# Fixed pieces of one tile and four double PSUM banks in place of tile pools, in a kernel with two spectral and two state-space layers

## The chip, the cores and the metric

The kernel runs on one core of one Trainium2 chip. The metric is the device time of one execution in microseconds (us), lower is better, as the median of several executions.

## The reference

An activation x of 2048 rows and 512 columns goes through four layers, each with a layer norm and a residual:

```
x = x + A(layernorm(x))
x = x + B(layernorm(x))
x = x + A(layernorm(x))
x = x + B(layernorm(x))

A(x):  irfft2(rfft2(x) * (w_r + 1j*w_i))                     # filter over both axes
B(u):  K[d,l] = Re sum_n C[d,n] * exp(dt*A[d,n]*l) * dt*B[d,n]
       irfft(rfft(pad(u)) * rfft(pad(K)))[:2048] + u*Dskip   # long convolution along the rows
```

All is float32. Both layers B use the same kernel K, so its spectrum is computed once.

## The kernel before

All Fourier transforms are matmuls with tables of cosines and sines, in two steps each, with the twiddle factors in the second step's table. A first part builds the spectrum of K (`setup_k`, 32 times `unit_k` on `exp_k`'s result, then `store_k`, `turn_k`, `spectra_k`); it needs x nowhere and runs beside the first layer A (index r = 0). Then follow layer B (r = 0), layer A (r = 1) and layer B (r = 1).

Layer A is `forward_a` (16 blocks of 128 rows), `first_a` or `group_a` (16 groups of frequencies) and `inv_a` (16 blocks). In `inv_a` four matmuls (L732) go to PSUM, ScalarE copies them out (L735), one matmul (L740) follows, ScalarE copies again (L743), and GpSimd and VectorE add the block to x.

Layer B is done in two column halves, e = 0 and e = 1.
- `forward_b`, 8 blocks b for each half: VectorE normalises two row blocks into a tile (L511), TensorE transforms them by eight matmuls (L781), four to each of two PSUM banks; ScalarE copies each bank out (L783), and the block is stored to DRAM in a new layout (L799, from SP's queue for even b, from ScalarE's for odd b). Matmuls of fp32 are in the trace with two records each, so a block of eight shows as x16. For r = 0 and e = 0 the two banks are one tile of 1024 elements, `pa`; else they are two tiles `px`.
- `group_b`, 16 groups q for each half: four matmuls to `px` (L811 and L812, with the tables `gi` and the rows of x's transform), two VectorE products with the spectrum `kh` (L873), two GpSimd sums (L879), four matmuls (L886) to the two banks `ph` and `pt`, and two ScalarE copies back (L892). For r = 0 and e = 1 the spectrum is computed in the same place from loads `yk` and `gk` (L853, L854) by matmuls on the same lines L811 and L812 and a copy (L860); else it is loaded (L864).
- `inv_b`, 8 blocks for each half: a load from DRAM (L901), eight matmuls to `ph` and `pt` (L908), and two VectorE adds to x (L914).
- `tables(r)` loads the 16 tables `gi` (L838), 256 KB each.

Nothing is written in a fixed order. Each of these functions is a generator whose pieces a list scheduler, the class `Clock`, takes one after the other: it keeps modelled times for each engine and takes the ready piece of the lowest rank. A piece yields what it needs before the next step: an engine, slots by name (`"PE p:h p:t"` is PE and a PSUM slot of the kinds h and t), and events. `Clock.tile` hands out the slot that the model takes to come free first; the order in which the pieces are taken is the order of the program on each engine's queue.

Memory is of two sorts. Some names are rings: fixed slices of tiles that stand for the whole program, with a table of sizes and counts for each (`RING`, `RINGA`, ...). The others (`a`, `iy`, `kh`, `yk`, `gk`, `KT`, `yh`, ...) and all of PSUM are allocated from tile pools, one new tile object for each use, with so many buffers for each tag. There are two such scopes one after the other, `w1` for the first 16 `forward_a` up to `forward_b` e = 0, and `w2` for all that follows. In PSUM `w1` has three double banks `a` and two single banks `s`; `w2` has four single banks `x`, two `t` and two `h`.

The waits on semaphores come from the framework: it compares the regions that each instruction reads and writes, and at the end of a pool's scope whatever takes its memory waits for all that used the pool.

Of the kernel before, what the change touches and what calls it, by code (L numbers as in the profile page):

```python
# [6 lines left out]
F32 = mybir.dt.float32  # L7
F32R = mybir.dt.float32r
BF = mybir.dt.bfloat16
# [1 line left out]
AF = mybir.ActivationFunctionType  # L11
OP = mybir.AluOpType

BUFS1 = {'yh': 3, 'KT': 3, 'st': 2, 'gb': 2}

RINGW = {"y": (514, 2), "b": (256, 2), "d": (256, 2), "c": (256, 2), "a": (512, 2)}
BUFS2 = {'a': 3, 'iy': 4, 'kh': 5, 'yk': 4, 'gk': 4}
BANKS1 = {'s': 2, 'a': 3}

SAME1, TWO = {'t': 's', 'h': 's', 'l': 's', 'x': 's', 'k': 'a'}, ('a',)  # L20
BANKS2 = {'t': 2, 'x': 4, 'h': 2}

RING = {"M": (3072, 3), "E": (3072, 2), "sq": (512, 2)}
RING0 = {"an": (3072, 1), "F": (2048, 1), "W": (1024, 2), "U": (1024, 2), "k": (512, 3), "hi": (1024, 2), "hj": (256, 2), "th": (512, 1), "ld": (4, 1),
         "dt": (4, 1)}
RINGX = {"G": (1284, 5), "t1a": (514, 1), "t2a": (514, 1), "Za": (520, 1)}

RINGG = {"G": (1798, 4), "tp": (128, 3)}
RINGA = {"G5": (1798, 1), "AB": (516, 3), "V": (516, 2), "t1a": (516, 2), "t2a": (516, 2), "Za": (516, 2)}
RINGB = {"gi": (512, 16)}  # L30

RINGC = {"b": (256, 3), "c": (256, 3), "d": (256, 3), "y": (512, 2), "yh": (512, 2)}
RINGD = {"t1": (512, 3), "t2": (512, 3), "Z": (512, 3)}
# [8 lines left out]
RANK = -4, 0.3, 6, 1.2, 25, 0.5, 24, 0.5  # L42

NEAR = 0.1


PSUM = bass.MemoryType.PSUM
# [4 lines left out]
MAGIC = 1.5 * 2.0 ** 23  # L52
# [130 lines left out]
class Clock:  # L183
# [4 lines left out]
    def __init__(self, net, last=None):  # L188
        self.net, self.n = net, len(net.nc.cur_bb.bb.instructions)
        self.free, self.seen, self.events, self.marks, self.drops = {}, {}, {}, [], []  # L190
        self.held, self.slots, self.land, self.piece, self.table, self.form = {}, {}, 0.0, None, "", None
        if last:
            self.free, self.seen, self.events, self.land, self.table = last.free, last.seen, last.events, last.land, last.table

            self.held = {k: h for k, h in last.held.items() if h[0] == "gi"}
            self.slots["gi"] = last.slots["gi"]

    def tile(self, name, make, count):

        slots = self.slots.setdefault(name, [(0.0, i) for i in range(count)])  # L200
        assert slots, name
        slots.sort()
        t, i = slots.pop(0)
        tile = make(i)
        self.held[self.key(tile)] = name, i, self.piece, tile
        if name not in self.net.ring:
            self.seen[tile.tensor.name] = [(self.boxes(tile), t, True)]
        return tile

    @staticmethod  # L210
    def key(tile):
        return tile.tensor.name, tile.offset * mybir.dt.size(tile.dtype)

    def drop(self, tile):
        self.drops.append(self.key(tile))
# [139 lines left out]
    def run(self, plan):  # L355

        pieces = [[rank, i, 0.0, (), piece] for i, (rank, piece) in enumerate(plan)]
        while pieces:
            ready = [(t, p) for p in pieces if (t := self.time(p[2], p[3])) is not None]
            assert ready, [p[4].__name__ for p in pieces]  # L360
            now = min(t for t, _ in ready) + NEAR
            t, p = min((e for e in ready if e[0] <= now), key=lambda e: e[1][:2])
# [13 lines left out]
class Net:  # L376
    def __init__(self, tc, io, ctx):
        self.tc, self.nc, self.io, self.ctx = tc, tc.nc, io, ctx
        self.const = self.pool("const", 1)
        self.big = self.pool("big", 1)  # L380
        self.ps = None
        nc = self.nc
        self.x = self.big.tile([128, 16, 512], F32, name="x")
        self.Ya = self.big.tile([128, 8192], F32, name="Ya")
        self.Y = self.big.tile([128, 16384], F32, name="Y")

        self.Yf = self.Ya, self.Y[:, :8192]

        self.place = [a.rearrange("p (g m) -> p g m", g=16) for a in (self.Y[:, 8192:], self.Ya)]
        self.eps = self.const.tile([128, 1], F32, name="eps")  # L390
        nc.vector.memset(self.eps, 1e-5)
        self.sm = self.pool("sm", 4)
        self.wk = None

    def pool(self, name, bufs, space=None):
        kw = {"space": space} if space is not None else {}
# [7 lines left out]
    def psum(self, kind):  # L404
        kind = self.same.get(kind, kind)

        def make(_):
            return self.ps.tile([128, 1024 if kind in TWO else 512], F32, name="p" + kind, tag="p" + kind, bufs=self.banks[kind])
        return self.timer.tile("p:" + kind, make, self.banks[kind])

    def drop(self, *tiles):

# [10 lines left out]
    def emitted(self, key, n=1):  # L423
        return self.timer.emitted(key, n)

    def work(self, name, bufs, **banks):

        net = self

        class Scope:  # L430
            def __enter__(scope):
                scope.cm = net.tc.tile_pool(name=name, bufs=1)
                net.wk = scope.cm.__enter__()
                scope.pm = net.tc.tile_pool(name=name + "p", bufs=1, space=PSUM)
                net.ps = scope.pm.__enter__()
                net.banks, net.bufs = banks, bufs

            def __exit__(scope, *a):
                net.wk = net.ps = None
                scope.pm.__exit__(*a)  # L440
                return scope.cm.__exit__(*a)
        return Scope()

    def w(self, name, shape, dt=F32):
        if name in self.ring:
            t = self.ring[name]
            t = self.timer.tile(name, t.__getitem__, len(t))
            t = t[:shape[0], :int(np.prod(shape[1:]))]
            if len(shape) > 2:
                names = "abcdef"[:len(shape) - 1]  # L450
                t = t.rearrange(f"p ({' '.join(names)}) -> p {' '.join(names)}", **dict(zip(names, shape[1:])))
            return t
        bufs = self.bufs.get(name, 1)

        def make(_):
            return self.wk.tile(list(shape), dt, name=name, tag=name, bufs=bufs)
        return self.timer.tile(name, make, bufs)


    def loads(self):  # L460
# [370 lines left out]

    def tables(self, r):

        for q in range(16):
            yield "SP gi", self.emitted(("inverse", 1), 16) if r else self.after("product", 32)
            self.gi[r, q] = self.w("gi", [128, 4, 128])
            self.timer.keep(self.gi[r, q])
            self.nc.sync.dma_start(self.gi[r, q], self.io["cGb"][q])  # L838
            self.mark("gi", r, q)
# [97 lines left out]
        self.nc.sync.dma_start(self.an[:, 2:6], self.io["kN"][:, 2:6])  # L937

    def load_h(self):
        cs = self.wk.tile([128, 5120], F32, name="cs")  # L940
        self.ring["yd"] = [cs[:, 1024 * i:1024 * i + 1024] for i in range(5)]
        self.ring["co"], self.ring["si"] = self.ring["yd"][:3], self.ring["yd"][3:]
        self.oh = self.wk.tile([128, 2560], BF, name="oh")[:96]
        self.nc.sync.dma_start(self.oh, self.io["cH"])

    def turns_of(self, out, t, n, k):
# [225 lines left out]
    def run(self):  # L1172
        self.khat = self.pool("khat", 1, DRAM).tile([128, 16, 2, 512], F32, name="khat")
        self.spe = self.pool("spe", 1, DRAM).tile([3, 2, 128, 1024], BF, name="spe")
        self.spt = self.pool("spt", 1, DRAM).tile([3, 128, 512], BF, name="spt")
        self.sq, self.st, self.gi = {}, {}, {}
        self.kd = self.pool("kd", 1, DRAM).tile([4, 4, 2048, 32], F32, name="kd")
        self.yk = self.pool("yk", 1, DRAM).tile([2, 16, 8, 4, 4, 2, 256], F32, name="yk")
        self.ring = {}
        self.same = SAME1  # L1180
        with self.work("w1", BUFS1, **BANKS1):
            wa = self.wk.tile([128, 3588], F32, name="wa")

            self.nc.vector.memset(wa[:, 64:64 + 514 + 1:514], 0.0)
            self.rings((RINGB, self.Y), (RING, self.Y), (RING0, self.Y), (RINGX, self.x.rearrange("p s d -> p (s d)")), (RINGW, wa))
            for name, value in (("magic", MAGIC), ("quarter", np.pi / 2)):
                t = self.const.tile([128, 1], F32, name=name)
                self.nc.vector.memset(t, value)
                setattr(self, name, t)
            sb = {}  # L1190
            self.timer = Clock(self)
            self.timer.run([(0, self.loads()), *self.plan_k(), *self.plan_a(sb)])
        self.same = {}
        with self.work("w2", BUFS2, **BANKS2):
            wb = self.wk.tile([128, 4608], F32, name="wb")
            self.ring = {"gi": self.ring["gi"]}
            self.rings((RINGG, self.Y[:, 8192:]), (RINGA, self.Ya), (RINGC, wb), (RINGD, wb))
            self.ring["G"] += self.ring.pop("G5")
            self.timer = Clock(self, self.timer)
            self.timer.run(self.plan_rest(sb))  # L1200

    def rings(self, *tables):

# [128 lines left out]
```

## Time and profile before

| | |
|---|---|
| median of 3 executions | 912.03 us (908.24 to 914.18) |
| profiled execution | 911.37 us |
| span of its trace | 909.6 us |
| mean granted TensorE clock | 0.941 |
| TensorE matmul busy | 711.0 us (78%) |
| TensorE weight loads | 501.4 us (55%, beside the matmuls) |
| VectorE busy | 562.9 us (62%) |
| ScalarE busy | 443.2 us (49%) |
| GpSimd busy | 374.2 us (41%) |
| DMA engines, queues of SP and ScalarE | 40.4% and 11.3% |

The span is shorter than the time by 1.8 us, which lie around it. Rows of the trace name a line (L886), an engine, the operation, and the tiles written and read with the shapes; "[9.35 <-X]" is the idle time of the engine ahead of the row, and what ended it.

### The profile page before, as it was taken

Reading aid. Unit: us, or ns where it says so; the run is one execution under the profiler, and the core shown is the slowest. Engines: PE = TensorE matmul, PEld = TensorE weight load, DVE = VectorE, ACT = ScalarE, POOL = GpSimd, SP = SyncE. Lnnn points to the kernel's source line nnn. Section 1 sums busy time; section 2 is a strip of 40 time slices with the busy share of each in tenths; the row PEclk is TensorE's granted clock in tenths of the full one; section 3 lists DMA queues with packets and bytes.
Section 4 is the critical chain, followed back from the end, with each engine's and each line's share of the span. In section 5 each row is a group of like instructions: output and inputs, shape, how many; then the busy total and the mean of one; then the engine's idle time right before and its main releaser. Section 6 shows DMA issues by size and latency. Waiting matters only on the chain.

```text
span 909.6 us, 17039 instructions
## 1 busy us (share of the span) xinstructions
PE 711.0 (78%) x6434; PEld 501.4 (55%) x6434; DVE 562.9 (62%) x1094; ACT 443.2 (49%) x817; POOL 374.2 (41%) x420
## 2 busy tenths in 40 slices
PE   0058888678878988973899978897887978599977
PEld 0046665355555645641656745696676645366646
DVE  6986887477475758761344534695884857566432
ACT  2458878776757667641344213286442444322210
POOL 0046665274353546631134215273443633166330
PEclk9999999999989889996899999899998989999998
DMA  9042025413413854557978994802540144767938
GB/s 327 32 148 75 13 78 185 122 61 123 155 53 128 267 135 132 175 163 173 272 190 235 260 347 140 216 3 78 207 163 1 47 93 127 181 200 197 268 85 228
DMA packets 91856, 138.39 MB, mean 152 GB/s; under 512 B 6812, under 2 KB 61344, under 8 KB 91136
## 3 DMA queue, kind: packets, MB, share of 16 engines
q1 hardware_dynamic: 59520, 107.95, 40.4%
q10 hardware_dynamic: 32256, 29.37, 11.3%
q8 instruction: 51, 0.84, 0.4%
q14 instruction: 29, 0.24, 0.1%
HBM read 76.60 MB, written 27.13 MB: 114 GB/s over the span
## 4 chain that ended last, share of the span: by engine, by line
PE 29%; DMA 9%; DVE 5%; ACT 3%; POOL 2%; issue 2%; SPq 1%; ACTq 0%; DVEq 0%; POOLq 0%
PE ph L886 6%; PE px L811 4%; PE px L781 3%; PE ph L908 3%; PE pt L732 3%; DMA iy<-Y 3%; PE px L812 3%; DMA Y<-iy 3%; DMA iy<-Ya 2%; DMA gk<-in_cGk_dram 2%; POOL Ya L622 1%; PE ph L740 1%; PE ph L631 1%; DVE Ya L617 1%; DVE Ya L618 1%
## 5 line engine op out<-in xcount | busy, mean ns | idle before, releaser
L879 POOL TENSOR_TENSOR wb<-wb 128x256 f32<-128x256 f32 x128 | 89.7, 729 | 159.2 <-DVE wb L873 119.7
L873 DVE TENSOR_TENSOR wb<-px,kh 128x512 f32<-128x512 f32 x128 | 80.9, 685 | 83.8 <-PE px L812 32.4
L1084 POOL TENSOR_TENSOR Y<-cs,Y 128x1024 f32<-128x1024 f32 x32 | 76.7, 2397 | 62.2 <-issue 29.6
L908 PE MATMUL ph<-iy,cRbT 64*128 64x256 f32 x256 | 67.2, 411 | 15.9 <-DMA iy<-Ya 13.3
L886 PE MATMUL ph<-wb,Y 64*128 64x256 f32 x256 | 70.9, 400 | 1.7 <-POOL wb L879 1.6
L886 PE MATMUL pt<-wb,Y 64*128 64x256 f32 x256 | 71.5, 401 | 0.0
L908 PE MATMUL pt<-iy,cRbT 64*128 64x256 f32 x256 | 66.5, 410 | 0.9 <-DVE x L914 0.9
L908 PEld LDWEIGHTS ph<-iy,cRbT 64*128 64x128 f32 x256 | 49.6, 202 | 25.2 <-issue 14.4
L781 PE MATMUL px<-a,cRb 128*64 128x256 f32 x384 | 50.8, 406 | 14.5 <-DMA Y<-in_cGb_dram 9.4
L886 PEld LDWEIGHTS ph<-wb,Y 64*128 64x128 f32 x256 | 42.7, 186 | 27.8 <-POOL wb L879 17.0
L1037 PE MATMUL pa<-oh,Y 96*128 96x512 bf16 x128 | 39.9, 389 | 22.9 <-DVE Y L1081 9.3
L1069 DVE SCALAR_TENSOR_TENSOR cs<-cs,pa 128x1024 f32<-128x1024 f32 x32 | 38.9, 1215 | 30.3 <-ACT cs L1067 30.1
L550 PE MATMUL ps<-cRa,wa 128*128 128x128 f32 x64 | 13.5, 294 | 55.9 <-POOL wa L535 55.2
L783 ACT COPY iy<-px 128x512 f32<-128x512 f32 x48 | 28.1, 586 | 56.8 <-PE px L781 56.7
L1080 DVE TENSOR_TENSOR Y<-pa,Y 128x1024 f32<-128x1024 f32 x32 | 39.0, 1219 | 21.9 <-ACT pa L1073 21.8
L908 PEld LDWEIGHTS pt<-iy,cRbT 64*128 64x128 f32 x256 | 49.9, 202 | 4.5 <-DVE x L914 3.1
L781 PEld LDWEIGHTS px<-a,cRb 128*64 128x64 f32 x384 | 32.9, 145 | 32.4 <-issue 16.5
L1072 ACT ACTIVATE cs<-cs,quarter 128x1024 f32<-128x1024 f32 x32 | 36.7, 1148 | 24.4 <-DVE cs L1070 22.6
L1053 ACT ACTIVATE Y<-pa 128x1024 f32<-128x1024 f32 x48 | 47.1, 1044 | 1.8 <-PE pa L1037 1.2
L914 DVE TENSOR_TENSOR x<-x,ph 128x256 f32<-128x256 f32 x32 | 13.4, 420 | 53.5 <-PE pt L908 43.0
L1097 PEld LDWEIGHTS ps<-Y 128*32 128x32 f32 x2048 | 33.8, 119 | 18.1 <-POOL Y L1085 8.5
L886 PEld LDWEIGHTS pt<-wb,Y 64*128 64x128 f32 x256 | 42.7, 186 | 0.2
(233 smaller groups left out, 1981.2 us busy)
## 6 DMA issues: line engine op xcount, KB each, us to landing
kh<-khat SPq DMA_DIRECT2D x48, 256.0 KB
Y<-in_cGb_dram SPq DMA_DIRECT2D x32, 256.0 KB
iy<-Y SPq DMA_DIRECT2D x16, 512.0 KB
iy<-Ya SPq DMA_DIRECT2D x16, 512.0 KB
Y<-in_W_dram SPq DMA_DIRECT2D x13, 515.0 KB
x<-in_cPa_dram SPq DMA_DIRECT2D x16, 384.0 KB
yk<-yh ACTq DMA_DIRECT2D x24, 256.0 KB
Y<-in_cGa_dram SPq DMA_DIRECT2D x13, 384.0 KB
```

The costliest lines, as they stand in the source:

```text
L781: self.nc.tensor.matmul(p[64 * s:64 * s + 64, 256 * h:256 * h + 256], self.Rb[:, 2 * h + j, :], xn[s], start=True, stop=True)
L811: self.nc.tensor.matmul(Xr[o], gb[:, j, 0:64], y[:, j, :], start=True, stop=True)
L873: nc.vector.tensor_tensor(t[c], X[:, c, None, :].to_broadcast([128, 2, 256]), k, op=OP.mult)
L879: nc.gpsimd.tensor_tensor(Z[:, c], t[0][:, c], t[1][:, c], op=op)
L886: nc.tensor.matmul(v[j], gi[o, 2 + c, :], Z[o, c, :], start=c == 0, stop=c == 1)
L908: nc.tensor.matmul(q[s], self.RbT[o, i, :], y[o, i, :], start=i == 0, stop=i == 3)
L1037: self.nc.tensor.matmul(p, f[:, c:c + 128], self.oh[:k, o:o + 512], start=True, stop=True)
L1053: nc.scalar.activation(m[:, :, 1024:] if i == 2 else m[:, i, :1024], p.rearrange("p (i m) -> p i m", i=2) if i == 2 else p, AF.Exp)
L1069: nc.vector.scalar_tensor_tensor(s, c, MAGIC, p, op0=OP.subtract, op1=OP.subtract)
L1072: nc.scalar.activation(c, c, AF.Sin, scale=-TURN, bias=self.quarter)
L1080: nc.vector.tensor_tensor(E[:, 1, :1024], p, m[:, :1024], op=OP.mult)
L1084: nc.gpsimd.tensor_tensor(E[:, 0, :1024], c, m[:, :1024], op=OP.mult)
```

## The change

The pools of the two scopes go. One tile `wk` of 128 x 17152 floats and four PSUM tiles `ps` of 128 x 1024 floats (two banks each) are allocated once. All names become rings on `wk`: RING1 behind RINGW for the first stage, RINGC, RINGD (one over the other) and RING2 for the second. Three counts grow: `gb` from 2 to 3 slots, `yk` and `gk` from 4 to 5. A single PSUM bank is now the left or the right half of a double tile: `s` the halves of the tile 3; `x` the four halves of the tiles 0 and 1, `t` those of the tile 2, `h` those of the tile 3. With one tile for both stages there is no end of a pool between them; an instruction of the second stage waits for those of the first whose regions it overlaps. In `tables` the condition is asked once, ahead of the loop, and the "+" in the yield lets each load follow the last without waiting for the modelled landing of the one before.

```diff
-BUFS1 = {'yh': 3, 'KT': 3, 'st': 2, 'gb': 2}
+RING1 = {"yd": (1024, 5), "oh": (1280, 1), "KS": (2048, 1), "KT": (512, 3), "yh": (512, 3), "gb": (256, 3), "st": (256, 2), "sk": (128, 1)}
...
-BUFS2 = {'a': 3, 'iy': 4, 'kh': 5, 'yk': 4, 'gk': 4}
-BANKS1 = {'s': 2, 'a': 3}
-
-SAME1, TWO = {'t': 's', 'h': 's', 'l': 's', 'x': 's', 'k': 'a'}, ('a',)
-BANKS2 = {'t': 2, 'x': 4, 'h': 2}
+RING2 = {"a": (512, 3), "iy": (1024, 4), "kh": (512, 5), "yk": (512, 5), "gk": (256, 5), "sk": (128, 1)}
+
+BANKS1, SAME1 = {'a': (0, 2, 4), 's': (6, 7)}, {'t': 's', 'h': 's', 'l': 's', 'x': 's', 'k': 'a'}
+BANKS2 = {'x': (0, 1, 2, 3), 't': (4, 5), 'h': (6, 7)}
...
         self.held[self.key(tile)] = name, i, self.piece, tile
-        if name not in self.net.ring:
-            self.seen[tile.tensor.name] = [(self.boxes(tile), t, True)]
         return tile
...
-        self.ps = None
+        self.ps = [self.pool("ps", 1, PSUM).tile([128, 1024], F32, name="ps%d" % i) for i in range(4)]
+        self.wk = self.big.tile([128, WORK], F32, name="wk")
...
     def psum(self, kind):
         kind = self.same.get(kind, kind)
 
-        def make(_):
-            return self.ps.tile([128, 1024 if kind in TWO else 512], F32, name="p" + kind, tag="p" + kind, bufs=self.banks[kind])
-        return self.timer.tile("p:" + kind, make, self.banks[kind])
+        banks = self.banks[kind]
+
+        def make(i):
+            p = self.ps[banks[i] // 2]
+            return p if kind == "a" else p[:, 512 * (banks[i] % 2):512 * (banks[i] % 2) + 512]
+        return self.timer.tile("p:" + kind, make, len(banks))
...
+        yield self.emitted(("inverse", 1), 16) if r else self.after("product", 32)
         for q in range(16):
-            yield "SP gi", self.emitted(("inverse", 1), 16) if r else self.after("product", 32)
+            yield "+SP gi"
             self.gi[r, q] = self.w("gi", [128, 4, 128])
```

The instructions are the same but for one table load on ScalarE. Their order differs between about 170 and 560 us of the trace; behind that, in layer A (r = 1) and layer B (r = 1), each of the four computing engines has the same order as before, and only the slots and the waits differ.

On SP's queue at the end of the first stage (line numbers of the changed kernel are lower by 21 to 24: L838 is L817, L799 is L777, L864 is L843, L1115 is L1091, L1126 is L1102) there stood

```order
L838 DMA Y<-in_cGb_dram 128x512 x2
L1115 DMA kd<-KS 128x2048
L838 DMA Y<-in_cGb_dram 128x512 x3
L799 DMA Y<-cs 16x8x1024
L838 DMA Y<-in_cGb_dram 128x512
...
L838 DMA Y<-in_cGb_dram 128x512 x8
L1126 DMA yk<-kd 128x4x128
L864 DMA kh<-khat 128x2x256 x3
```

(where the line of dots stands, the pair of one L799 and one L838 comes twice more, and then a fourth L799), and now

```order
L817 DMA Y<-in_cGb_dram 128x512 x16
L1091 DMA kd<-wk 128x2048
L777 DMA Y<-wk 16x8x1024 x4
L1102 DMA wk<-kd 128x4x128
L843 DMA wk<-khat 128x2x256 x3
```

All 16 tables now stand ahead of the four stores of `forward_b` blocks; before, eight of them stood behind the last.

On TensorE the last two blocks of `forward_b`, r = 1, with the tiles' numbers and the semaphores that each row waits for, stood before as

```order
L781 MATMUL px_6361<-a_6354,cRb_158 64x256 [waits DVE_49,Activation_49]
L781 MATMUL px_6361<-a_6354,cRb_158 64x256 [waits DVE_49]
L781 MATMUL px_6361<-a_6354,cRb_158 64x256 x2
L781 MATMUL px_6362<-a_6354,cRb_158 64x256 [waits Activation_49]
L781 MATMUL px_6362<-a_6354,cRb_158 64x256 x3
```

and now as

```order
L759 MATMUL ps0_66<-wk_79,cRb_166 64x256 [waits DVE_49] x2
L759 MATMUL ps0_66<-wk_79,cRb_166 64x256 x2
L759 MATMUL ps0_66<-wk_79,cRb_166 64x256 [waits Activation_49]
L759 MATMUL ps0_66<-wk_79,cRb_166 64x256 x3
```

The matmuls are the same and in the same order. Before, the second four write a tile of their own, and their wait on ScalarE is for the copy that emptied that bank an earlier time; now both fours write halves of the one tile ps0, and by its value the second four's wait on ScalarE is for the copy of the first four's result in the other half (the copy that the block's first four release).

More of the change, by code (lines that the diff above doesn't have):

```diff
@@ L44 @@
 NEAR = 0.1
+WORK = 17152
 PSUM = bass.MemoryType.PSUM
@@ L392, in __init__ @@
         self.sm = self.pool("sm", 4)
-        self.wk = None
     def pool(self, name, bufs, space=None):
@@ L424, in emitted @@
         return self.timer.emitted(key, n)
[L426 to L442, printed above, removed]
-    def w(self, name, shape, dt=F32):
[L445 to L457, printed above, removed]
+    def w(self, name, shape, dt=F32):
+        t = self.ring[name]
+        t = self.timer.tile(name, t.__getitem__, len(t))
+        t = (t if dt is F32 else t.bitcast(dt))[:shape[0], :int(np.prod(shape[1:]))]
+        if len(shape) > 2:
+            names = "abcdef"[:len(shape) - 1]
+            t = t.rearrange(f"p ({' '.join(names)}) -> p {' '.join(names)}", **dict(zip(names, shape[1:])))
+        return t
     def loads(self):
@@ L939, in load_h @@
     def load_h(self):
[L940 to L943, printed above, removed]
+        self.oh = self.ring["oh"][0].bitcast(BF)[:96]
         self.nc.sync.dma_start(self.oh, self.io["cH"])
@@ L1179, in run @@
         self.ring = {}
[L1180 to L1200, printed above, removed]
+        self.banks, self.same = BANKS1, SAME1
+        n = sum(n * k for n, k in RINGW.values())
+        self.nc.vector.memset(self.wk[:, 64:64 + 514 + 1:514], 0.0)
+        self.rings((RINGB, self.Y), (RING, self.Y), (RING0, self.Y), (RINGX, self.x.rearrange("p s d -> p (s d)")), (RINGW, self.wk),
+                   (RING1, self.wk[:, n:]))
+        self.ring["co"], self.ring["si"] = self.ring["yd"][:3], self.ring["yd"][3:]
+        for name, value in (("magic", MAGIC), ("quarter", np.pi / 2)):
+            t = self.const.tile([128, 1], F32, name=name)
+            self.nc.vector.memset(t, value)
+            setattr(self, name, t)
+        sb = {}
+        self.timer = Clock(self)
+        self.timer.run([(0, self.loads()), *self.plan_k(), *self.plan_a(sb)])
+        self.banks, self.same = BANKS2, {}
+        self.ring = {"gi": self.ring["gi"]}
+        n = sum(n * k for n, k in RINGD.values())
+        self.rings((RINGG, self.Y[:, 8192:]), (RINGA, self.Ya), (RINGC, self.wk), (RINGD, self.wk), (RING2, self.wk[:, n:]))
+        self.ring["G"] += self.ring.pop("G5")
+        self.timer = Clock(self, self.timer)
+        self.timer.run(self.plan_rest(sb))
     def rings(self, *tables):
```

## The prediction

> **What bounds the kernel now.** I first read the windows, the busy time of each engine by 40 us (start and end; PE, PEld, DVE, ACT, POOL with instruction counts; granted TensorE clock; DMA share; GB/s), because the change lies in several stages with different limits.
>
> ```profile
> 400.00:440.00 40.00, 20.10 (x127) 12.01 (x125) 9.01 (x26) 9.78 (x18) 2.28 (x3) 0.71 0.81 202
> 440.00:480.00 40.00, 38.60 (x268) 23.17 (x266) 17.46 (x31) 16.42 (x38) 14.17 (x21) 0.99 0.87 219
> 480.00:520.00 40.00, 39.51 (x329) 28.46 (x327) 19.30 (x37) 12.94 (x32) 15.22 (x22) 1.00 0.93 257
> 800.00:840.00 40.00, 39.85 (x320) 25.52 (x319) 25.33 (x41) 11.64 (x36) 28.63 (x41) 1.00 0.75 216
> 880.00:910.00 30.00, 17.82 (x132) 15.09 (x128) 6.02 (x16) 0.65 (x2) 0.00 (x0) 0.86 0.83 210
> ```
>
> Both layers B (440 to 560 and 796 to 866 us) are bound by TensorE: it is busy for 38.6 to 39.9 of 40 us, so whatever makes it wait there is added to the end nearly in full. Between them lies the boundary of the two stages, 400 to 440, the worst stretch: TensorE is busy for half of it. The tail from 880 is set by loads (DMA share 0.83) and has slack on TensorE.
>
> The timeline there, by engine (start, duration, engine, line, tiles, count, idle time ahead and its end):
>
> ```profile
> 423.34 0.54 SPq L799 DMA_DIRECT2D Y<-cs  x1
> 423.93 10.54 SPq L838 DMA_DIRECT2D Y<-in_cGb_dram  x8
> 434.61 2.03 DVE L511 TENSOR_SCALAR a<-x,mv,rs 128x256 f32<-128x256 f32 x6 [15.95 <-DMA Y<-in_cGb_dram]
> 435.12 9.92 PE L781 MATMUL px<-a,cRb 128*64 128x256 f32 x64 [9.35 <-DMA Y<-in_cGb_dram]
> 444.72 0.75 PE L811 MATMUL px<-Y 128*64 128x256 f32 x4
> ```
>
> The first instruction of the second stage, L511 into `a`, waits 15.95 us, TensorE then 9.35. The last even store leaves at 423.34, eight table loads behind it. The program of before makes L511 wait for all that used the first stage's pool, the last stores among them.
>
> **The boundary: a gain.** In the changed program L511 waits only for the stores whose regions it overlaps, of which that of 423.34 is the last, and the 16 tables have gone ahead of it. How long a store of this size takes without those loads is in the chain of waits (start, us, what), at the end of layer A (r = 1), which I need again below:
>
> ```profile
> 716.00 1.90 PE px L781 x16
> 725.07 3.63 PE px L781 x32
> 728.73 0.59 ACT iy L783
> 734.55 4.32 DMA Y<-iy
> ...
> 786.37 3.91 PE px L781 x31
> ...
> 790.31 5.25 DMA Y<-iy
> ...
> 795.69 1.13 PE px L811 x4
> ```
>
> So the store lands at about 423.34 + 4.32 = 427.7, and L511 starts 434.61 - 427.7 = 6.9 us earlier. Before, four `forward_b` blocks (x64) then stand ahead of the first L811; in the new order only two, each 9.92 / 4 = 2.48 us here, so L811 comes 6.9 + 5.0 = 11.9 us earlier. The two others are paid later, at 1.9 us each (the row x16 at 716.00): 11.9 - 3.8 = **8 us gained**. Bounds: 2 us, if the spectra `kh`, which are loaded behind the same stores, come late; 12, if the two blocks fall into holes. At the second boundary the store of 790.31 took 5.25 us beside three table loads that now stand ahead of it; at 4.32 it gives **1 us**. Together -9.
>
> [...]
>
> **PSUM halves: a loss.** Each single bank is now half of a tile, and the program's waits go by tile: an instruction that touches one half waits for another engine's last access to the other half too. By resolving the semaphore values of both built programs I count 585 waits whose instruction named touches only the other part of a PSUM tile, against 139 before. The trace of before already shows what one costs, since `pa`, the double tile of `forward_b` (r = 0, e = 0), has it and `px` does not. The groups (busy us, mean ns, idle us ahead and what ended it), the waits (us, times, longest) and a piece of the timeline:
>
> ```profile
> L781 PE MATMUL px<-a,cRb 128*64 128x256 f32 x384 | 50.8, 406 | 14.5 <-DMA Y<-in_cGb_dram 9.4 <-DVE a L511 5.2
> L781 PE MATMUL pa<-wa,cRb 128*64 128x256 f32 x128 | 19.6, 429 | 12.2 <-DVE wa L511 6.7 <-ACT cs L783 5.5
> PEld pa L781 <- ACT cs L783: 9.5, 8, 1.5
> 402.32 1.95 PE L781 MATMUL pa<-wa,cRb 128*64 128x256 f32 x16 [0.69 <-ACT cs L783]
> ```
>
> With `pa`, 8 blocks lose 5.5 us of matmul time to the copy of their own first half, 0.69 each; with `px`, 24 blocks lose none to it. [...]
>
> Now by line, with the copies' and adds' groups:
>
> ```profile
> L892 ACT COPY Y<-ph 128x256 f32<-128x256 f32 x32 | 11.9, 373 | 49.1 <-PE pt L886 47.7 <-ACT iy L1146 1.2 <-PE ph L886 0.2
> L914 DVE TENSOR_TENSOR x<-x,ph 128x256 f32<-128x256 f32 x32 | 13.4, 420 | 53.5 <-PE pt L908 43.0 <-PE ph L908 10.4
> L557 ACT COPY Ya<-ps 128x512 f32<-128x512 f32 x16 | 16.7, 1051 | 5.1 <-PE ps L553 5.0
> ```
>
> `forward_b`: the 24 `px` blocks now behave as `pa`. Eight (r = 0, e = 1) lie in the stretch where TensorE is the bound: 8 x 0.69 = 5.5. Of the 16 of r = 1, 12 are in the chain of waits (10 pieces, the first and the last of them at 716.00 and 786.37): 12 x 0.69 = 8.3. **+14**; bounds 5.5 (the first eight alone) and 24 x 0.69 = 16.6.
>
> `group_b`: here the timeline decides, at 816 us, where two groups follow each other and then a product:
>
> ```profile
> 816.06 0.48 PE L886 MATMUL ph<-wb,Y 64*128 64x256 f32 x1
> 817.03 0.38 PE L886 MATMUL ph<-wb,Y 64*128 64x256 f32 x1
> 817.22 0.37 ACT L892 COPY Y<-ph 128x256 f32<-128x256 f32 x1 [1.44 <-PE pt L886]
> 817.68 0.38 PE L886 MATMUL pt<-wb,Y 64*128 64x256 f32 x1
> 818.36 0.38 ACT L892 COPY Y<-pt 128x256 f32<-128x256 f32 x1
> 819.01 0.48 PE L886 MATMUL ph<-wb,Y 64*128 64x256 f32 x1
> 829.30 1.29 DVE L873 TENSOR_TENSOR wb<-px,kh 128x512 f32<-128x512 f32 x2 [1.66 <-POOL wb L879]
> 830.18 0.66 PE L811 MATMUL px<-Ya,Y 128*64 128x256 f32 x4
> ```
>
> The copies of the first group, begun at 817.22, now wait for the second group's matmuls in the other half, till 817.68 + 0.38 = 818.06, and the last of the four copies ends some 0.6 us later than at 818.74; the next group's start at 819.01 moves by about 0.3. Where a product stands between groups, as usual, nothing is lost. The other new wait is L811 for L873's reads of the other half: 829.30 + 1.29 = 830.59 against 830.18, 0.4 us. Over 812 to 832 us I find three such delays of TensorE, 0.4 to 0.7, in 9 groups: 1.7 / 9 = 0.2 each. For all 64 groups **+13**. Bounds: 0, and both copies in full ahead of every group, 64 x 2 x 0.375 = 48; I stay near the stretch counted.
>
> `inv_b`: 24 of 32 blocks now wait for the adds of the block before in the other half, at most 0.42 + 0.40 us. Half of them lie in the tail, which the loads set. **+4**; bounds 0 and 24 x 0.82 = 20.
>
> The first stage and layer A (r = 1): `s` is two halves of one tile, so `forward_a`, `first_a`, `inv_a` and the units lose some of their double buffering (L550 waits for L557's copy of the other half, 1.05 us, in 14 places, the copy for L553 in 15). But TensorE is less full there,
>
> ```profile
> 240.00:280.00 40.00, 31.19 (x414) 21.67 (x414) 25.32 (x38) 26.15 (x34) 18.30 (x12) 0.91 0.16 46
> 640.00:680.00 40.00, 33.70 (x286) 28.09 (x282) 33.82 (x92) 17.70 (x67) 18.26 (x27) 0.96 0.57 197
> ```
>
> 31 and 34 of 40 us, so that part falls into idle time, and the order up to 440 is another, which may help or hurt. **+5**; bounds -5, and 29 x 1.05 = 30.
>
> More slots for `yk` and `gk`: the chain holds one wait on a load,
>
> ```profile
> 530.07 9.86 DMA gk<-in_cGk_dram
> 540.06 1.13 PE px L811 x4
> ```
> ```profile
> L811 PE MATMUL px<-yk,gk 128*64 128x256 f32 x64 | 10.9, 408 | 5.5 <-DMA gk<-in_cGk_dram 5.5
> ```
>
> for which TensorE idles 5.5 us (the group's row). The load's place on SP is the same, behind the layer A loads; I take 0, bounds -5.5 and 0. `gb` lies in the first stage's terms. What the scheduler no longer notes for fresh tiles changes only the order.
>
> **Sum:** -9 + 14 + 13 + 4 + 5 = +27 us on the profiled execution's 911.4, 938; the median of the runs is 912.0, 0.6 above, so **939**.
>
> **Rivals.** *The waits are hidden.* The copies are short beside ScalarE's idle time (L892's group: 49 us idle), and TensorE, ordered as before, may find them done. For it speaks that most groups have a product between them; against it the 0.69 us of each `pa` block, on the chip. Then the boundary decides: 912 - 9 = 903, and 898 with the `gk` wait gone. Chance 0.13. [...]
> *They cancel.* `forward_b` alone is paid (14) and the rest half: -9 + 14 + 6 = +11 at most, down to -9; 903 to 921. The same time comes if the fixed pieces release no sooner than the pools, with the waits as cheap. Chance 0.22.
> *The waits chain.* A late copy delays a group, this the product, the product's bank the next: with `forward_b` in full and half of the other upper bounds (17 + 24 + 10 + 15 = 66, less 9) the time is 969; from there on this rival has decided. For it speaks that TensorE has no slack in layer B; against it the single pair above, where one delay of 0.3 is absorbed by the next product. Chance 0.07.
> The forecast, slower by 921 to 969, has 0.58.
>
> A measurement of this kernel can hardly tell less than 1% (9 us) from none. Faster by more: 0.13; within: 0.22; slower: 0.65. The range 903 to 970 leaves out the first rival and most of the third, 0.19.
>
> **What will show it.** In the changed trace: L511 behind the boundary near 428, with an idle time ahead of TensorE's first `forward_b` block there of some 2 to 3 us and not 9.35; a row for `forward_b` on the PSUM halves with idle time that ends on ScalarE's copy L783 (now L761), 24 times 0.69; in 440 to 560 and the last layer B TensorE's busy time per 40 us down by 1 to 3 us; new waits of L886's group on L892's. If the stretch after the boundary to the end is no longer than before, the halves cost nothing and I am wrong; if the first stage ends more than 10 us from 411, the order there was what mattered.

## The result, and the profile after

The changed kernel takes 1024.0 us (1022.5 to 1031.2, 4 runs) against 913.1 before (908.2 to 914.3, 4 runs): a ratio of 1.124 with a 95% interval of 1.117 to 1.131. The forecast was slower, by 27 us; it became slower by 111. The profiled execution took 1031.2 us, with a span of 1029.4 and a granted clock of 0.912 against 0.941.

The windows of the changed kernel, in the columns of before; the first layer B now reaches from 482 to 630 and the last from 904 on:

```profile
440.00:480.00 40.00, 21.24 (x96) 9.70 (x94) 13.47 (x33) 9.21 (x19) 6.97 (x9) 0.62 0.54 133
520.00:560.00 40.00, 32.60 (x256) 19.61 (x254) 13.19 (x22) 13.41 (x32) 12.70 (x18) 1.00 0.71 196
560.00:600.00 40.00, 32.49 (x230) 21.71 (x230) 17.11 (x38) 5.49 (x14) 6.98 (x10) 0.96 0.79 249
920.00:960.00 40.00, 36.91 (x276) 24.11 (x276) 18.78 (x34) 8.87 (x28) 18.27 (x26) 1.00 0.74 199
1000.00:1040.00 40.00, 23.59 (x128) 18.82 (x128) 6.01 (x16) 0.00 (x0) 0.00 (x0) 0.82 0.56 141
```

In the first layer B TensorE is now busy for 32 to 33 of 40 us where it was for 39; in the last for 37 where it was for 40. Summed over the span (the engines' row of the page):

```profile
PE 758.4 (74%) x6434; PEld 512.5 (50%) x6434; DVE 550.0 (53%) x1094; ACT 443.5 (43%) x818; POOL 373.5 (36%) x420
```

The same 6434 records of matmuls are busy for 758.4 us in place of 711.0. So of the 120 us by which the span grew, TensorE idles 72 longer (1029.4 - 758.4 = 271.0 against 909.6 - 711.0 = 198.6), and for 47 the same matmuls take longer.

The growth lies in all stretches but the boundary. From the first matmul of `forward_a` to the end of the last `forward_b` block of the first stage TensorE takes 412.5 us in place of 370.6 (41.9 more); from there to the first product 15.0 in place of 19.0 (4.0 less); to the first `forward_a` of layer A (r = 1) 171.0 in place of 139.3 (31.7 more: the first layer B); to the first group of the last layer B 250.9 in place of 216.9 (34.0 more: layer A and `forward_b`); and to the end of TensorE's work 121.3 in place of 104.8 (16.5 more: the last layer B).

The boundary, as far as it answers to the rows of before (L489 is L511 of before, L759 is L781, L761 is L783, L789 is L811):

```profile
468.90 1.38 DVE L489 TENSOR_SCALAR wk<-x,mv,rs 128x256 f32<-128x256 f32 x4 [9.72 <-ACT wk L761]
469.37 2.29 PE L759 MATMUL ps<-wk,cRb 128*64 128x256 f32 x8 [1.80 <-DVE wk L489]
476.79 0.59 ACT L761 COPY wk<-ps 128x512 f32<-128x512 f32 x1 [8.56 <-DMA Y<-wk]
477.42 3.51 PE L759 MATMUL ps<-wk,cRb 128*64 128x256 f32 x16 [5.76 <-ACT wk L761]
482.54 0.65 PE L789 MATMUL ps<-Y 128*64 128x256 f32 x4
```

TensorE's first block behind the boundary waits 1.80 us in place of 9.35: the release works. But its second half waits 5.76 more, for the copy of its first half, and that copy waits for the last store of the first stage, over whose memory the block's output lies. And `forward_b` by group and wait:

```profile
L759 PE MATMUL ps<-wk,cRb 128*64 128x256 f32 x512 | 78.5, 436 | 39.2 <-ACT wk L761 28.1 <-DVE wk L489 10.6 <-DVE wk L852 0.6
PE ps L759 <- ACT wk L761: 28.1, 26, 5.8
PEld ps L759 <- ACT wk L761: 42.7, 27, 6.6
```

The idle time that ends on the block's own copy has grown from 5.5 to 28.1 us, in 26 waits: 24 of them some 0.7 us long, one of 5.76 at the boundary and one of 5.52 in r = 1.

### The profile page after: what moved, and what is told of

Same layout as the page of the kernel before. It is cut to its first block, busy times and chain, and to the rows that moved or that the text cites. A ratio compares the mean times of both kernels' runs of the same rounds, so it can differ in the third digit from the quotient of the medians.

```text
span 1029.4 us, 16968 instructions
## 1 busy us (share of the span) xinstructions
PE 758.4 (74%) x6434; PEld 512.5 (50%) x6434; DVE 550.0 (53%) x1094; ACT 443.5 (43%) x818; POOL 373.5 (36%) x420
## 5 line engine op out<-in xcount | busy, mean ns | idle before, releaser
L858 POOL TENSOR_TENSOR wk<-wk 128x256 f32<-128x256 f32 x128 | 89.7, 729 | 192.3 <-DVE wk L852 181.3
L852 DVE TENSOR_TENSOR wk<-ps,wk 128x512 f32<-128x512 f32 x128 | 80.9, 685 | 103.9 <-issue 34.7
L1060 POOL TENSOR_TENSOR Y<-wk,Y 128x1024 f32<-128x1024 f32 x32 | 77.1, 2410 | 91.0 <-ACT wk L1048 70.3
L759 PE MATMUL ps<-wk,cRb 128*64 128x256 f32 x512 | 78.5, 436 | 39.2 <-ACT wk L761 28.1
L887 PE MATMUL ps<-wk,cRbT 64*128 64x256 f32 x512 | 81.2, 430 | 18.1 <-DMA wk<-Ya 10.7
L865 PE MATMUL ps<-wk,Y 64*128 64x256 f32 x512 | 75.9, 405 | 11.0 <-POOL wk L858 5.1
L887 PEld LDWEIGHTS ps<-wk,cRbT 64*128 64x128 f32 x512 | 60.8, 209 | 38.0 <-DVE x L893 14.6
L528 PE MATMUL ps<-cRa,wk 128*128 128x128 f32 x128 | 28.4, 307 | 69.4 <-POOL wk L513 55.1
L759 PEld LDWEIGHTS ps<-wk,cRb 128*64 128x64 f32 x512 | 38.3, 152 | 80.0 <-ACT wk L761 42.7
L761 ACT COPY wk<-ps 128x512 f32<-128x512 f32 x64 | 37.5, 586 | 88.0 <-PE ps L759 79.4
L865 PEld LDWEIGHTS ps<-wk,Y 64*128 64x128 f32 x512 | 48.5, 188 | 39.4 <-POOL wk L858 23.4
L513 POOL TENSOR_TENSOR wk<-wk 128x256 f32<-128x256 f32 x32 | 24.2, 756 | 104.6 <-DVE wk L489 54.4
L528 PEld LDWEIGHTS ps<-cRa,wk 128*128 128x128 f32 x128 | 21.1, 207 | 74.7 <-POOL wk L513 56.5
L1045 DVE SCALAR_TENSOR_TENSOR wk<-wk,ps 128x1024 f32<-128x1024 f32 x32 | 38.9, 1216 | 34.6 <-ACT wk L1043 34.5
L871 ACT COPY Ya<-ps 128x256 f32<-128x256 f32 x64 | 20.4, 378 | 75.6 <-PE ps L865 52.0
L489 DVE TENSOR_SCALAR wk<-x,mv,rs 128x256 f32<-128x256 f32 (+1 forms) x80 | 35.0, 476 | 32.5 <-PE ps L759 15.5
L1029 ACT ACTIVATE Y<-ps 128x1024 f32<-128x1024 f32 x48 | 46.6, 1033 | 5.2 <-PE ps L1013 4.0
L1013 PE MATMUL ps<-wk,Y 96*128 96x512 bf16 x128 | 41.5, 410 | 9.5 <-DVE Y L1057 4.5
```

The lines of the kernel that those rows point to most:

```text
L528: nc.tensor.matmul(o, pq[:, 0, :], self.Ra, start=True, stop=False)
L759: self.nc.tensor.matmul(p[64 * s:64 * s + 64, 256 * h:256 * h + 256], self.Rb[:, 2 * h + j, :], xn[s], start=True, stop=True)
L852: nc.vector.tensor_tensor(t[c], X[:, c, None, :].to_broadcast([128, 2, 256]), k, op=OP.mult)
L858: nc.gpsimd.tensor_tensor(Z[:, c], t[0][:, c], t[1][:, c], op=op)
L865: nc.tensor.matmul(v[j], gi[o, 2 + c, :], Z[o, c, :], start=c == 0, stop=c == 1)
L887: nc.tensor.matmul(q[s], self.RbT[o, i, :], y[o, i, :], start=i == 0, stop=i == 3)
```

## The experiments

H below is that waits between the halves of a PSUM tile make the loss, O that the changed order does, W that the one tile `wk` does.

**e1: PSUM from pools again, the rest as changed.**

```diff
-            return p if kind == "a" else p[:, 512 * (banks[i] % 2):512 * (banks[i] % 2) + 512]
-        return self.timer.tile("p:" + kind, make, len(banks))
+            return self.ps.tile([128, 1024 if kind == "a" else 512], F32, name="p" + kind, tag="p" + kind, bufs=self.banks[kind])
+        return self.timer.tile("p:" + kind, make, self.banks[kind])
```

> The changed kernel with PSUM alone put back: its tiles come from pools again, one tile for each use, and fresh tiles are noted by the scheduler as before; wk as one tile, its rings and the tables' loads stay changed. The order in the first stage is that of before. Theory H (waits between the two halves of a double PSUM tile make the loss): 900 to 908, that is before less the 8 us of the boundary. Rival O (the changed order in the first stage and in the first layer B): the same, 900 to 908. Rival W (waits on the one tile wk): over 1000, as the changed kernel.

Measured: 907.4 us against 912.0, a ratio of 0.994 (0.991 to 0.997). W falls; H and O both hold. Its boundary, and the last store ahead of the last layer B (L758 is L781 of before, L788 is L811):

```profile
429.23 5.21 PE L758 MATMUL px<-wk,cRb 128*64 128x256 f32 x32 [2.77 <-DVE wk L488]
434.34 2.05 ACT L760 COPY wk<-px 128x512 f32<-128x512 f32 x4 [7.22 <-PE px L758]
434.98 0.66 PE L788 MATMUL px<-Y 128*64 128x256 f32 x4 [0.54 <-ACT wk L760]
781.36 10.30 DMA Y<-wk
```

With no halves the product starts 9.7 us earlier than before (434.98 against 444.72). The copies wait here too: they begin at 434.34, when the first fours have long been done, and by the changed kernel's row it is the last store that they wait for. But both blocks' matmuls are then finished or nearly so, and the product follows at once. Against that, the store ahead of the last layer B takes 10.30 us and not 5.25.

**e2: the kernel before, with PSUM alone in halves of four double banks.**

```diff
-            return self.ps.tile([128, 1024 if kind in TWO else 512], F32, name="p" + kind, tag="p" + kind, bufs=self.banks[kind])
-        return self.timer.tile("p:" + kind, make, self.banks[kind])
+            p = self.ps[banks[i] // 2]
+            return p if kind == "a" else p[:, 512 * (banks[i] % 2):512 * (banks[i] % 2) + 512]
+        return self.timer.tile("p:" + kind, make, len(banks))
```

> The kernel before with PSUM alone changed: four double banks for the whole program, single banks are halves. Pools for the working tiles stay. Its order is that of the changed kernel in its last two thirds and nearly so ahead. Theory H: 1015 to 1040, about the changed kernel without its gain at the boundary. Rival O: much the same, as the order moves with it. Rival W: 905 to 920.

Measured: 1016.6 us, a ratio of 1.113 (1.106 to 1.120). This one part does the damage, but it moves the order too.

**e3: the changed kernel, banks 6 and 7 as two tiles; e4: all single banks as tiles.** The order on each engine's queue is instruction for instruction that of the changed kernel, and the tiles lie in the same banks.

```diff
+        self.ps1 = [self.pool("ps", 1, PSUM).tile([128, 512], F32, name="pt%d" % i) for i in range(2)]
...
+            if banks[i] > 5:
+                return self.ps1[banks[i] - 6][:, 0:512]
             p = self.ps[banks[i] // 2]
```

> The changed kernel with the fourth double tile split into two tiles of one bank (kinds s in the first stage, h in the second); the order of all instructions is exactly that of the changed kernel, but 400 waits name another part of a PSUM tile in place of 585. Theory H: the first stage gets most of its 42 us back and the groups of layer B a part: 960 to 990. Rival O: 1005 to 1024, since the order is unchanged. Rival W: 1024.

> The changed kernel, in exactly its order, with single banks as tiles of their own: in the first stage three double tiles and two single ones, in the second eight single ones from a second scope; 243 waits name another part of a PSUM tile. Theory H: 903 to 915, all of the loss gone. Rival O: 945 to 970, since the first stage's and the first layer B's order stay changed. Rival W: 1000 to 1024.

Measured: e3 982.5 us, 1.075 (1.071 to 1.079); e4 916.0 us, 1.003 (0.999 to 1.006). With the same instructions in the same order in the same banks, the waits alone are worth 1024 - 916 = 108 us. That settles H against O, of which at most 916.0 - 907.4 = 8.6 us is left (e1 differs from e4 in the order, and also in which bank each use gets). e4 came 1 us over the range expected.

How the first stage loses is seen best in `forward_a`, whose four-matmul pieces go to the two banks `s` in turn. The timeline of before (L550 and L553 matmuls, L557 the copy) and of the changed kernel (L528, L531, L535):

```profile
72.86 0.46 PE L550 MATMUL ps<-cRa,wa 128*128 128x128 f32 x2 [0.28 <-ACT wa L543]
73.45 1.11 ACT L557 COPY Ya<-ps 128x512 f32<-128x512 f32 x1
74.71 0.46 PE L550 MATMUL ps<-cRa,wa 128*128 128x128 f32 x2 [0.27 <-ACT wa L543]
```
```profile
80.69 1.02 ACT L535 COPY Ya<-ps 128x512 f32<-128x512 f32 x1 [0.85 <-PE ps L531]
81.86 0.46 PE L528 MATMUL ps<-cRa,wk 128*128 128x128 f32 x2 [1.20 <-POOL wk L514]
83.13 0.72 POOL L513 TENSOR_TENSOR wk<-wk 128x256 f32<-128x256 f32 x1 [1.34 <-issue]
83.47 1.02 ACT L535 COPY Ya<-ps 128x512 f32<-128x512 f32 x1 [0.84 <-PE ps L531]
84.64 0.46 PE L528 MATMUL ps<-cRa,wk 128*128 128x128 f32 x2 [1.20 <-POOL wk L514]
```

Before, the copy of one block (73.45 to 74.56) runs beside the next block's matmuls (those begun at 72.86), and a block takes 74.71 - 72.86 = 1.85 us. Afterwards each waits for the other: the copy begins when the matmuls end (0.84 idle for L531), the next matmul when the copy ends (83.47 + 1.02 = 84.49, and 84.64), and a block takes 84.64 - 81.86 = 2.78. The row puts this wait down to GpSimd's L514; by the program's semaphores L528 waits for the copy L535 and for L513, and L513 was done at 83.85. For all sixteen blocks, from the first matmul to the last, it is 46.8 us in place of 32.1, 15 more. At the end of the stage the changed kernel is 31 us behind e3, which has the same order and `s` in two tiles (467.57 and 436.80); so the other half is lost further on.

**e8 and e10: one kind in halves, all else single, same order.** e8 has only the four banks `x` of the second stage in halves, e10 only the two banks `s` of the first.

```diff
+            wide = [pool.tile([128, 1024], F32, name="pd%d" % b) for b in range(2)]
+            self.ps = [wide[b // 2][:, 512 * (b % 2):512 * (b % 2) + 512] for b in range(4)] + self.ps
```

> The experiment with all single banks (916) with only the four banks x of the second stage as halves of two double tiles; t and h stay single. Same order. The experiment with two single tiles has x and t in halves and takes 982, so x and t make 66 together. Theory X (x makes most: 24 blocks of forward_b at some 1.1 us, and the products that wait for reads of the other half): 955 to 970. Rival T (t makes most, by the groups): 925 to 940.

> The experiment with all single banks (916) with the two banks s of the first stage alone as halves of one tile; same order. Theory H, by the times at which the first stage ended (467.6 in the changed kernel, 436.8 with two single tiles): 916 + 31 = 947, at 940 to 952, all of it ahead of the second stage. Rival (part of it is taken up behind the first stage, where loads set the pace): 925 to 935.

Measured: e8 957.4 us, 1.048 (1.045 to 1.051); e10 948.9 us, 1.039 (1.033 to 1.045). Both are in the range of the first theory. So `x` costs 957.4 - 916.0 = 41 us, `t` 982.5 - 957.4 = 25, `s` 948.9 - 916.0 = 33, and `h` what is left, 1024.0 - 982.5 - 33 = 9, if the kinds add up. In e8's groups the waits that `x` in halves brings are (L758 is `forward_b`, L788 the product; `pd` the tiles in halves):

```profile
L758 PE MATMUL pd<-wk,cRb 128*64 128x256 f32 x384 | 59.9, 442 | 25.7 <-ACT wk L760 20.4 <-DVE wk L488 4.9 <-DVE wk L851 0.3
L788 PE MATMUL pd<-Y 128*64 128x256 f32 x128 | 23.1, 435 | 7.7 <-DVE wk L851 6.0 <-DMA Y<-wk 0.8 <-ACT wk L1121 0.8
L788 PE MATMUL pd<-Ya,Y 128*64 128x256 f32 x128 | 21.0, 399 | 8.7 <-DVE wk L851 7.9 <-ACT wk L838 0.9
L788 PE MATMUL pd<-wk 128*64 128x256 f32 x64 | 11.4, 429 | 4.7 <-ACT wk L838 4.3 <-DVE wk L851 0.3
```

20.4 for the copy of the block's own first half, in 18 of the 24 blocks, two of which wait 3.6 and 5.8 us; 14 for VectorE's reads of the other half (L851), and 5 for the copy of the spectrum (L838). These 40 us are not the 41 term by term: in e4's trace the same four groups idle 7.4, 14.2, 0 and 6.2 us for other waits, part of which the new ones take the place of, so that the groups idle 19 us more (25 more than in e1's trace). The rest is not seen in these rows.

**e7: t and h paired by group.** One line: the two banks that a group uses at the same time share a tile, and the next group has the other.

```diff
-BANKS2 = {'x': (0, 1, 2, 3), 't': (4, 5), 'h': (6, 7)}
+BANKS2 = {'x': (0, 1, 2, 3), 't': (4, 6), 'h': (5, 7)}
```

> The changed kernel with one table changed: in the second stage a double tile holds one bank h and one bank t (banks 4 and 6 for t, 5 and 7 for h), so that the two banks which one group or block uses at the same time share a tile, and the next group has the other tile. Order unchanged, 587 waits on another part of a tile. Theory H, as I now have it (a wait costs where the two halves belong to work that follows one another, little where they belong to the same): 995 to 1005 in place of 1024. Rival (each such wait costs alike, by their number): 1024.

Measured: 1002.6 us, 1.098 (1.095 to 1.101). The number of waits on another part of a tile is the same (587 against 585), yet 21 us go: what counts is not how many such waits there are but whether the other half belongs to the work that should overlap. Of `t` and `h` (34 together), 12 stay. The gain lies in the two layers B (156.8 us in place of 171.0, and 111.4 in place of 121.3); layer A (r = 1) stays at 250.

The end of both kernels shows a second price. After the last wait for a load TensorE has eight `inv_b` blocks of 16 records to do; the changed kernel, then e7:

```profile
1000.54 3.79 PE L887 MATMUL ps<-wk,cRbT 64*128 64x256 f32 x16 [5.42 <-DMA wk<-Ya]
1004.87 4.11 PE L887 MATMUL ps<-wk,cRbT 64*128 64x256 f32 x16 [0.54 <-DVE x L893]
1009.16 4.10 PE L887 MATMUL ps<-wk,cRbT 64*128 64x256 f32 x16 [0.18 <-DVE x L893]
1013.45 2.32 PE L887 MATMUL ps<-wk,cRbT 64*128 64x256 f32 x16 [0.20 <-DVE x L893]
1015.96 2.32 PE L887 MATMUL ps<-wk,cRbT 64*128 64x256 f32 x16 [0.18 <-DVE x L893]
...
1023.47 2.32 PE L887 MATMUL ps<-wk,cRbT 64*128 64x256 f32 x16 [0.18 <-DVE x L893]
```
```profile
981.41 11.27 PE L887 MATMUL ps<-wk,cRbT 64*128 64x256 f32 x80 [5.46 <-DMA wk<-Ya]
```

In e7 the first five blocks run without a gap and take 11.27 us. In the changed kernel the five take 17.74 (from 1000.54 to 1015.96 + 2.32), and only 1.1 of the 6.5 more are the gaps: three blocks run at nearly half the speed, 4.1 us in place of 2.3, for 13 us after the wait. The clock granted is 0.50 there, up to 1013, and 1.00 from 1014 to 1026. For e7 an estimate: in the tail of before the matmuls to one bank start 0.43 us apart at half clock and 0.22 at full, two records each time, so 80 records in 11.27 us leave some 5 us at half clock.

**e5, e6, e9: the other parts.** e6 is the kernel before with the run of tables for the first layer B alone; e9 the fixed pieces of `wk` alone; e5 is e1 with the tables of the last layer B paced as before.

```diff
+        if not r:
+            yield self.after("product", 32)
         for q in range(16):
-            yield "SP gi", self.emitted(("inverse", 1), 16) if r else self.after("product", 32)
+            yield ("SP gi", self.emitted(("inverse", 1), 16)) if r else "+SP gi"
```

> The kernel before with one part of the change alone: the tables of the first layer B are issued in one run; the pools and all else stay. Theory R (at the boundary the second stage waits for the pool's last stores, and of its 6.9 us about half is the tables in the stores' way): the last store, issued at 426.4, lands 4.4 later, at 430.8 against 434.6, so 908. Rival: the tables make all of it, 905. Rival: they make none, 912.

> The fixed pieces of wk alone: PSUM from pools and all tables' loads paced as before. At the boundary the second stage then waits for the stores that it overlaps and not for the pool's last ones, but the tables still stand behind the last even store. Theory (both parts of the boundary count, the tables more: alone they gave 0.8% in the experiment on the kernel before, and together with the pieces 1.0%): 907 to 911, under 1% faster than before. Rival (the order of the first stage, another in this kernel behind 300 us, costs what the boundary gives): 912 to 916.

> The first experiment's kernel (PSUM from pools, the rest as changed) with the tables' loads of the last layer B paced as before, each when the model has the last one landed; those of the first layer B stay in one run. In that kernel's trace the last store ahead of the last layer B takes 10.30 us behind 16 tables issued in one run, against 5.25 before. Theory Q (the run of tables delays that store, and all waits for it): 902, 5 less than its 907. Rival (the following products hide it): 907.

Measured: e6 907.6 us, 0.992 (0.989 to 0.995); e9 906.8 us, 0.992 (0.989 to 0.995); e5 905.1 us, 0.990 (0.987 to 0.994). All three are under 1% faster than before, and e9 came 0.2 us under its range. In time each of the two parts alone (e6, e9) gives as much as both together (e1, 907.4), but not at the boundary: the product comes 15.9 us behind the last block of the first stage in e6, 13.4 in e9 and 8.5 in e1, where before it came 19.0 behind. What e1 gains more there it has lost again by the last layer B. e6's boundary is nearly as theory R had it, L511 at 431.9 and not 434.6:

```profile
431.88 2.03 DVE L511 TENSOR_SCALAR a<-x,mv,rs 128x256 f32<-128x256 f32 x6 [13.91 <-DMA Y<-cs]
```

In e5 the store of the last layer B is back at

```profile
786.63 5.23 DMA Y<-wk
```

but of the 5 us hoped for the times show 2.4, and e1's and e5's intervals overlap; that the run of tables costs time there is seen in the store and not settled in the sum. e5, the change without the halves and with one run of tables, has the lowest median of all, but its interval overlaps those of e1, e6 and e9.

## Why the prediction was wrong in size

The direction and the kind of cause were right: the boundary gains, and waits between halves of a tile lose more. The steps that failed are two terms of the sum. The waits in the first stage and layer A, put at 5 us, were taken to fall into idle time; and the waits of `group_b` and `inv_b`, put at 17, were counted on a sample. In all the losses, 36 us in the sum, came to 1024.0 - 907.4 = 117.

- **The boundary** (-9). The first block starts 7.5 us sooner after the first stage's last one (1.8 us behind it, before 9.35), as forecast, and without the halves the product comes 9.7 us earlier, against 11.9. In the changed kernel it comes only 4 us sooner (15.0 us behind the last block of the first stage, 467.57 to 482.54, before 18.95), because with the half-tile wait of 5.76 us three of the four halves of the two blocks come behind the last store. The prediction took the store of 423.34 as the last that counts. That holds for the first L511; but the copy out of the first block, and through it the product, waits for the store behind that one, which leaves from ScalarE's queue (in e1 at 427.15). The 1 us at the second boundary was wrong in sign: I counted three tables that move ahead of the store, but all sixteen now do, in one run, and without the halves the store takes 10.30 us (e1), with the tables paced as before 5.23 (e5). The store leaves from ScalarE's queue and the tables from SP's, so being ahead in the order does not yet mean being out of the way: in e1 the sixteen are issued from 760.90 to 777.70, the store at 781.36, and still it takes 10.30.
- **`forward_b`** (+14, measured 22.6: 28.1 less 5.5). The price of 0.69 was right, the count was not. Of the eight blocks of r = 0, e = 1 only the two at the boundary paid, 5.76 and 0.69: the two banks of the other six lie in different tiles. All sixteen of r = 1 paid, not twelve: fourteen 0.7 each, one 1.07 and one 5.52. Before that one ScalarE itself stood idle for 5.60 us, by the trace for a load, and the copy came late.
- **`group_b` and `inv_b`** (+13 and +4). In the last layer B, whose order did not change, the first, the seventeenth and the last but one group of before and of the changed kernel start at

```profile
800.91 0.48 PE L886 MATMUL ph<-wb,Y 64*128 64x256 f32 x1
832.11 0.48 PE L886 MATMUL ph<-wb,Y 64*128 64x256 f32 x1
876.83 0.48 PE L886 MATMUL ph<-wb,Y 64*128 64x256 f32 x1 [0.27 <-POOL wb L879]
```
```profile
904.44 0.49 PE L865 MATMUL ps<-wk,Y 64*128 64x256 f32 x2
938.71 0.49 PE L865 MATMUL ps<-wk,Y 64*128 64x256 f32 x2
991.31 0.49 PE L865 MATMUL ps<-wk,Y 64*128 64x256 f32 x2
```

  Up to 832 us, which holds the stretch that I had counted, 16 groups lose 34.27 - 31.20 = 3.1 us, 0.19 each: the count was right. From there on 14 groups lose 52.60 - 44.72 = 7.9, 0.56 each; `inv_b` blocks stand between them there and use the same `h` and `t`, and with these paired by group (e7) the 52.60 are 48.41. The tail, which I held to be covered by loads, lost 5.6 us more (from there to the end of TensorE's work 905.71 - 876.83 = 28.9 and 1025.79 - 991.31 = 34.5; in e7 29.1). By an estimate from the windows most of that is the clock: TensorE is busy at half clock for 11.7 us there where it was for 5.3, half of the difference is 3.2. The first layer B, in which I had counted nothing, lost 31.7 us, nearly twice as much as the last. The stretch that I read was not like the rest: 48 us in all, not 17.
- **The first stage and layer A** (+5, and 33 for `s` alone, with 8.6 for the order beside it). This is the step that failed most. The first stage grew by 41.9 us, of which 31 go when `s` is two tiles (e3) and 11 stay with the order. Layer A (r = 1) with `forward_b` grew by 34.0, of which 16.2 are `forward_b`'s waits above; 7.5 are there in e1 too, without halves. I let the waits fall into TensorE's idle time, 31 to 34 of 40 us busy. But that idle time was the other half of the same chain: where matmul and copy alternate over two banks, one bank's copy fills the time of the other bank's matmuls, and with a wait between the banks the two add up (1.85 to 2.78 us for a block). The bound that I had written, 30, was about what `s` cost. The sign that I gave for the order, a first stage that ends more than 10 us from 411, came true (451.7 for the same block), and yet it was the halves and not the order that made most of it.
- **More slots** (0) held: in e5, with the five slots for `yk` and `gk`, the wait on `gk` is still there, 7.8 us and not 5.5 (in e1, with the same slots, 2.5).

```profile
L788 PE MATMUL px<-wk 128*64 128x256 f32 x64 | 11.4, 424 | 7.8 <-DMA wk<-in_cGk_dram 7.8
```

- **The clock.** No term of the sum had it. 47 us of the growth are matmuls that take longer. By the traces' records of the granted clock, which begin at 58 us and 71 us, TensorE was busy for 85 us at half clock before and for 141 in the changed kernel; half of the difference, 28 us, is by this estimate (0.43 us from start to start at half clock in the tail of before, 0.22 at full) the clock's part of the 47, without what lies ahead of the records. The rest was not separated.
- **Rivals.** "The waits chain" had 0.07, from 969 on; that is the time that came, in part at the place that the prediction named for it (a product behind a late group), and as much in the first stage, where it had no chain in mind. "The waits are hidden" is refuted, and its time, 903, is near what the kernel takes without the halves (905 to 907). The `pa` blocks that the prediction set against it were the better sign. The banks themselves need none of these waits: in the same banks and the same order e3 takes 982.5 us and e4 916.0, where the changed kernel takes 1024.0; the program waits because it counts by tile.
- **The count of waits.** 585 against 139 compared unlike things, since before each use has a tile of its own and the ordinary release of a bank is not counted. With a tile for each bank (e4) 243 are left, so 342 were new: 108 / 342 = 0.3 us each on average.

## What to carry to other kernels

Where the waits of a program go by tile, two buffers that are to overlap must be two tiles; two halves of one tile are one buffer (1024.0 us here, 916.0 with a tile for each bank). If halves must share a tile, pair those that the same step uses together (e7, 1002.6). When a wait is added to a chain, idle time on its engine covers it only if it belongs to another chain (in `forward_a` it did not, and 1.85 us for a block became 2.78): follow the two steps that alternate and add them up, and take the whole stretch, not a sample, for the count.

## What the runs showed of the hardware that was not expected

In two stretches with short waits the matmuls stayed slow for longer than without them. After an idle time of 5.43 us they run at about half speed in the kernel before for 5.3 us (granted clock 0.50 up to 891) and then at full speed (1.00 from 892), as the starts show (0.43 us apart till 890.98, then 0.22),

```profile
885.72 0.76 PE L908 MATMUL ph<-iy,cRbT 64*128 64x256 f32 x1 [5.43 <-DMA iy<-Ya]
890.55 0.63 PE L908 MATMUL ph<-iy,cRbT 64*128 64x256 f32 x1
890.98 0.44 PE L908 MATMUL ph<-iy,cRbT 64*128 64x256 f32 x1
891.25 0.38 PE L908 MATMUL ph<-iy,cRbT 64*128 64x256 f32 x1
```

but in the changed kernel, after 5.42 us and with gaps of 0.54 and 0.18 us every 4 us, for 13 (0.50 up to 1013). In e7, which has the same order and no such gaps, it is some 5 by the estimate above. It is the same at the start, where `forward_a`'s first blocks wait 1.20 us every 4.1 us: a matmul record takes 0.42 us there until 70, and 0.28 from 71.8 on. In the kernel before, whose order is the same there and whose blocks wait 0.25 us at most up to 66, it takes 0.42 until 57.8 and 0.28 from 58.3 on; in e3, also without the 1.20, the records of 55 to 104 us take 0.28 to 0.30 us on average, and in the changed kernel 0.31 to 0.33. In these pairs it is the waits that differ and not the order. Over the whole trace the records have half clock for 182 us where it was 109, and the mean granted clock is 0.912 against 0.941. Which gaps do this is open: behind 1013 the clock stays at 1.00 with gaps of 0.18 to 0.20. What each gap adds was not tried.
